# Two groups of six inner tiles in the channel mixer, and three VectorE-turned pairs in the second batch

## The chip, the cores and the metric

The kernel runs on one core of one Trainium2 chip. The metric is the device time of one execution in microseconds (us); the time of the kernel before is a median of three runs.

## What is computed

Three blocks follow each other, for a batch of 4 sequences of 448 positions. All inputs are float32, except the mixer's four weight matrices, which come as float64.

```
attention: 12 heads of 64; q, k rms-normed; softmax(q k^T / 8) v     -> x (4, 448, 768)
mixer:     u = x + (relu(x^T w_tok1) w_tok2)^T      w_tok1 448x256, w_tok2 256x448
           y = u + relu(u w_ch1) w_ch2              w_ch1 768x1536, w_ch2 1536x768
experts:   4 causal heads on y, gated by the 2 best of 4 logits, each with its own wo
```

## The kernel before

Heads are handled two at a time ("pairs"): six pairs (b,0) to (b,5) for each batch b. Every matrix product of the mixer is made of three matmuls on values split in two halves (high and low), 448 columns each, so that a product over K tiles of 128 is 3K matmuls on TensorE (PE), all recorded at L517.

**A pair's attention.** The scores (L599) come in two steps of two row blocks, VectorE (DVE) takes their maxima (L569), ScalarE (ACT) the exponentials (L584). The result must be turned before it can be multiplied with v (L722, "attend"). There are two ways. *Narrow* pairs are turned on PE: 28 transposes (L623) into four accumulators, which ACT or DVE copy out (L428 or L429). *Wide* pairs are turned by DVE: four stream transposes of 128x896 (L697), after which 16 copies between partition groups (L709), each on ACT, DVE or, for four of them, GpSimd (POOL), put the blocks in place. `LATE` names the first wide pair: every pair from it on, in order, is wide.

**The channel mixer** (`channel`, one call a batch). The 12 inner tiles of 128 are taken in `NG` groups of `GC`. For each group, PE makes `GC` inner tiles `hid` (L1088, 18 matmuls each: `a<-uhl,whl`), ACT or DVE takes relu (L433, L434), DVE the low half (L1095); then for each of the six output tiles PE makes a product over the group (L1102, 3 x GC matmuls: `a<-hid,whl`), which DVE adds to `u` (L1106). `RING` gives the number of buffers of a tile's ring: five for `hid`, six for the weights `whl`.

**Weights.** In the first batch each weight block is loaded as float64, in two halves (`narrow`): ACT takes two passes (L462, L465) and DVE two (L467, L469) to make float32 of a half; then `split` makes the high part (L428 or L429) and the low part (L447, on DVE or POOL) of each half, and both are stored in DRAM (L506). Later batches load the stored halves (L508).

**Order.** Every step has a cost and a list of engines that may run it. A list scheduler (`Plan.order`) lays all steps of the program out in time, chooses an engine where there is a choice, and the instructions are issued in that order. So a changed number moves rows on every engine. The pairs of batch b+1 are scored and turned while PE is in `channel(b)`: the pairs of batch 1 lie beside the first channel mixer, where the weights are prepared too. After it come the projection of batch 0 (`project`, L1123 and L1135) and the token mixer of batch 1, which needs the attention of all of batch 1's pairs.

Of the kernel before, what the change touches and what calls it, by code (L numbers as in the profile page):

```python
# [20 lines left out]


RING = {
    "w3": 3, "wraw": 2, "whl": 6, "hid": 5, "u": 6, "uhl": 6, "nat": 1,
# [17 lines left out]

FAST = {(0, 0), (0, 1)}

LATE = (1, 5)


class Buf:
# [268 lines left out]
def kernel(  # L317
# [40 lines left out]
    def sbuf(shape, dtype, tag):  # L358
        return plan.buf(sb, shape, dtype, tag, RING.get(tag, 1))
# [485 lines left out]
    class Stats:  # L845


        def __init__(self, b, qs, ks):
            n, m = len(qs), len(ks)
            self.b, self.qs, self.ks = b, qs, ks  # L850
            R = P if (b, max(qs + ks)) >= LATE else CP
            st = self.st = sbuf([R, 3, 64], F32, "st")
# [48 lines left out]
        def q(self, pr):  # L901
            o = self.at(0, pr)
            R = P if (self.b, pr) >= LATE else CP
            return self.st, lambda: self.st.t[:R, 1, o : o + 8].rearrange(
# [24 lines left out]
    class Pair:  # L929
# [10 lines left out]
        def stack(self):  # L940
# [3 lines left out]
            b, pr = self.b, self.pr  # L944
            wide = self.wide = (b, pr) >= LATE
            v = self.v = sbuf([P, NCH, 2, D], F32, "v")
# [279 lines left out]
def _layout(i):  # L1226
    import numpy as np

    b, h, s, d = i["q"].shape
    x = np.stack([i["q"], i["k"], i["v"]], axis=1).reshape(b, 3, h // 2, 2, s, d)  # L1230
    chunks = lambda y: y.reshape(b, h // 2, 2, 4, s // 4, d).transpose(0, 1, 4, 2, 3, 5)
    rows = lambda y: y.reshape(b, h // 2, 2, s // 4, 4, d).transpose(0, 1, 3, 2, 4, 5)
    kn = rows(x[:, 1]).copy()
    for at in FAST:
        kn[at] = chunks(x[:, 1])[at]
    qn = chunks(x[:, 0]).copy()
    late = [(i, j) for i in range(b) for j in range(h // 2) if (i, j) >= LATE]
    for at in late:
        qn[at] = rows(x[:, 0])[at]
    nat = np.stack([qn, kn], axis=3).reshape(b, h // 2, s // 4, 2, 2 * 4, d)  # L1240
    ends = [(0, 512 - s), (0, 0)]
    v = np.pad(x[:, 2], [(0, 0)] * 3 + ends)
    v[:, :, 1] = np.pad(x[:, 2, :, 1], [(0, 0)] * 2 + [ends[0][::-1], (0, 0)])
    vals = v.reshape(b, h // 2, 2, 4, 128, d).transpose(0, 1, 4, 3, 2, 5)
    qkt = x[:, :2].transpose(0, 2, 1, 3, 5, 4).reshape(b, h // 2, 2, 2 * d, s).copy()
    for at in late:
        qkt[at][0] = qkt[at][0].reshape(-1, s // 4, 4).swapaxes(-1, -2).reshape(-1, s)
    qkt = np.pad(qkt, [(0, 0)] * 4 + [(0, 16)])
    g = np.stack([i["g_q"], i["g_k"]], axis=1)
    gg = np.concatenate([g, g], axis=0)  # L1250
    t1, t2, c1, c2 = (
        np.ascontiguousarray(i["moe_w_" + n]).view(np.int64)
        for n in ("tok1", "tok2", "ch1", "ch2")
    )
    wt1 = t1.reshape(4, s // 4, -1).transpose(1, 0, 2).reshape(s // 4, -1)
    wt2 = t2.reshape(-1, 128, s).transpose(1, 0, 2).reshape(128, -1)
    dm, dc = c1.shape
    nd, ncc = dm // 128, dc // 128
    wc1 = c1.reshape(nd, 128, ncc, 128).transpose(2, 1, 0, 3).reshape(ncc, 128, dm)
    ng = 3  # L1260
    wc2 = (
        c2.reshape(ng, ncc // ng, 128, nd, 128).transpose(0, 3, 2, 1, 4)
        .reshape(ng, nd, 128, dc // ng)
    )
    e = i["moe2_wq"].shape[0]
    w = np.stack([i["moe2_wq"], i["moe2_wk"]], axis=0)
    w = w.reshape(2, e // 2, 2, nd, 128, d).transpose(1, 0, 4, 3, 2, 5)
    wqk = w.reshape(e, 128, dm)
    wv = i["moe2_wv"].transpose(1, 0, 2).reshape(dm, e * d)
    wvg = np.concatenate([wv, i["moe2_w_gate"]], axis=1)  # L1270
    wvg = wvg.reshape(nd // 2, 2, 128, -1).transpose(0, 2, 1, 3).reshape(nd // 2, 128, -1)
    wo = (
        i["moe2_wo"].reshape(e // 2, 2 * d, 2, dm // 2).transpose(2, 1, 0, 3)
        .reshape(2, 2 * d, e // 2 * (dm // 2))
    )
    return dict(nat=nat, qkt=qkt, vals=vals, gg=gg, wt1=wt1, wt2=wt2, wc1=wc1, wc2=wc2,
                wqk=wqk, wvg=wvg, wo=wo)
# [27 lines left out]
```

## Time and profile before

| | |
|---|---|
| time, median of 3 runs | 861.91 us (861.23 to 862.3) |
| profiled execution: time, span | 864.12 us, 862.3 us |
| PE busy | 823.4 us (95%) |
| DVE busy | 619.5 us (72%) |
| ACT busy | 468.0 us (54%) |
| POOL busy | 149.8 us (17%) |
| granted TensorE clock | full in all 40 slices |

The span is the time from the first to the last instruction of the profiled execution. Busy times are unions over an engine's instructions. The shares are means over stages that differ: the first 117 us (first batch's attention), the first channel mixer with the weights' preparation and the second batch's pairs (117 to 254 us), its projection, then three more rounds of the same with stored weights.

### The profile page before, as it was taken

The numbers are of one execution on the slowest core, as the hardware profiler recorded it, in microseconds if no ns is written. First come the engines' busy times: TensorE is split into PE (matmuls) and PEld (weight loads), VectorE is DVE, ScalarE is ACT, GpSimd is POOL, SyncE is SP. The second block draws the span as 40 slices with busy tenths as digits, with TensorE's granted clock in tenths as the row PEclk, the third lists the DMA queues.
The fourth block names the chain that finished last, engine by engine and source line by source line (L and its number), as shares of the span: only waits on it lengthen the run. The fifth ranks groups of instructions, "written<-read, shape, count | busy, mean of one in ns | idle before, by whom it ended". The sixth has DMA issues, their size and how long they took to land.

```text
span 862.3 us, 13533 instructions
## 1 busy us (share of the span) xinstructions
PE 823.4 (95%) x4564; PEld 636.1 (74%) x4564; DVE 619.5 (72%) x1341; ACT 468.0 (54%) x1077; POOL 149.8 (17%) x167
## 2 busy tenths in 40 slices
PE   3989999999989998999999998999999999999998
PEld 1446588777666876877776786788866789998786
DVE  6888988999999778646799877874389772125452
ACT  6898865577667546324395655641187631102443
POOL 3235640011123022020031211321031010000000
PEclk9999999999999999999999999999999999999999
DMA  8557769889878917687665614687656226676344
GB/s 249 165 156 208 221 187 297 275 266 308 254 230 230 312 67 233 187 270 233 174 192 158 188 47 138 206 224 209 197 160 160 91 71 186 211 239 206 106 136 165
DMA packets 109925, 168.40 MB, mean 195 GB/s; under 512 B 18112, under 2 KB 76608, under 8 KB 109856
## 3 DMA queue, kind: packets, MB, share of 16 engines
q1 hardware_dynamic: 109712, 167.54, 64.2%
q8 instruction: 36, 0.59, 0.3%
q14 instruction: 33, 0.27, 0.1%
q10 hardware_dynamic: 144, 0.00, 0.0%
HBM read 136.66 MB, written 30.84 MB: 194 GB/s over the span
## 4 chain that ended last, share of the span: by engine, by line
PE 73%; DVE 14%; DMA 5%; ACT 5%; issue 2%; SPq 0%; POOL 0%; ACTq 0%; DVEq 0%
PE a L517 52%; PE s L599 8%; PE m L722 8%; DVE nm L569 3%; ACT s L584 2%; PE m L748 2%; DMA w<-in_wc_dram 1%; DMA nat<-in_nat_dram 1%; PE s L647 1%; DVE wraw L467 1%; ACT s L428 1%; DVE s L709 1%; PE s L623 1%; DVE s L697 1%; DMA whl<-kept_c 1%
## 5 line engine op out<-in xcount | busy, mean ns | idle before, releaser
L517 PE MATMUL a<-uhl,whl 128*128 128x448 f32 x1152 | 242.5, 365 | 5.6 <-ACT ot L428 3.5
L517 PEld LDWEIGHTS a<-uhl,whl 128*128 128x128 f32 x1152 | 213.4, 188 | 35.2 <-issue 10.0
L517 PE MATMUL a<-hid,whl 128*128 128x448 f32 x864 | 187.0, 368 | 3.6 <-POOL whl L447 1.5
L517 PEld LDWEIGHTS a<-hid,whl 128*128 128x128 f32 x864 | 158.9, 188 | 31.1 <-issue 7.7
L584 ACT ACTIVATE s<-s,nm,st 128x448 f32<-128x448 f32 (+1 forms) x192 | 137.0, 724 | 65.1 <-DVE nm L575 41.8
L599 PE MATMUL s<-k,q 64*112 64x448 f32 (+4 forms) x512 | 112.4, 552 | 9.3 <-ACT s L584 6.6
L569 DVE TENSOR_REDUCE nm<-s 128x2 f32<-128x896 f32 (+1 forms) x96 | 101.7, 1082 | 10.4 <-PE s L599 10.1
L433 ACT ACTIVATE hid<-a 128x448 fp32r<-128x448 f32 x44 | 23.9, 543 | 131.1 <-PE a L517 131.0
L1095 DVE SCALAR_TENSOR_TENSOR hid<-a,hid 128x448 fp32r<-128x448 f32 x48 | 29.9, 622 | 75.8 <-ACT hid L433 75.5
L709 ACT COPY s<-s 32x896 f32<-32x896 f32 (+1 forms) x92 | 76.2, 829 | 9.8 <-DVE s L697 7.3
L722 PE MATMUL m<-s,v 128*64 128x448 f32 x384 | 77.5, 545 | 2.1 <-DVE s L709 1.1
L599 PEld LDWEIGHTS s<-k,q 64*112 64x112 f32 (+1 forms) x512 | 41.0, 184 | 48.8 <-issue 22.6
L1106 DVE TENSOR_TENSOR u<-a,u 128x448 f32<-128x448 f32 x72 | 44.3, 617 | 41.8 <-PE a L517 41.4
L447 POOL TENSOR_TENSOR uhl<-u,uhl 128x448 fp32r<-128x448 f32 x23 | 26.9, 1175 | 250.9 <-ACT uhl L428 131.5
L697 DVE STREAM_TRANSPOSE s<-s 128x896 f32<-128x896 f32 x52 | 55.6, 1094 | 14.1 <-ACT s L584 11.5
L709 DVE COPY s<-s 32x896 f32<-32x896 f32 (+1 forms) x87 | 59.9, 689 | 1.4
L722 PEld LDWEIGHTS m<-s,v 128*64 128x64 f32 x384 | 26.2, 136 | 44.0 <-issue 40.8
L584 ACT ACTIVATE s<-s,nm 112x112 f32<-112x112 f32 (+3 forms) x64 | 30.8, 492 | 28.3 <-DVE nm L563 28.1
L709 POOL COPY s<-s 32x896 f32<-32x896 f32 (+1 forms) x29 | 25.6, 882 | 94.6 <-DVE inv L669 53.5
L462 ACT ACTIVATE wraw<-w 128x256 f32<-128x256 f32 (+3 forms) x72 | 33.4, 464 | 15.6 <-DMA w<-in_wc_dram 15.3
L428 ACT ACTIVATE s<-s 112x448 f32<-112x448 f32 (+5 forms) x65 | 32.2, 539 | 16.2 <-PE s L647 11.2
L517 PE MATMUL a<-whl,uhl 128*112 128x260 f32 x288 | 39.9, 289 | 0.4 <-DVE q L545 0.4
(147 smaller groups left out, 1095.0 us busy)
## 6 DMA issues: line engine op xcount, KB each, us to landing
whl<-kept_c SPq DMA_DIRECT2D x72, 384.0 KB
whl<-kept_c SPq DMA_DIRECT2D x108, 256.0 KB
w<-in_wc_dram SPq DMA_DIRECT2D x24, 384.0 KB
kept_c<-whl SPq DMA_DIRECT2D x24, 384.0 KB
w<-in_wc_dram SPq DMA_DIRECT2D x36, 256.0 KB
kept_c<-whl SPq DMA_DIRECT2D x36, 256.0 KB
whl<-kept_qk SPq DMA_DIRECT2D x24, 384.0 KB
nat<-in_nat_dram SPq DMA_DIRECT2D x19, 448.0 KB
```

The lines of the kernel that those rows point to most:

```text
L428: lambda e: nc.scalar.activation(dst(), src(), AF.Copy) if e == "ACT"
L447: either(n, reads, writes, lambda e: e.tensor_tensor(dst()[:, 1], src(), f(dst()[:, 0]), op=ALU.subtract))
L462: add("ACT", act_ns(n), [(d, 1)], [(r, part)], lambda: nc.scalar.activation(rf(), half(1).bitcast(F32), AF.Copy, scale=2.0 ** -112))
L517: nc.tensor.matmul(acc, lhs[:, x], rhs[:, y], start=first and i == 0, stop=last and i == 2)
L569: lambda e: e.tensor_reduce(nm.t[:R, c], pst.t[:R, :, :w], axis=AX.X, op=ALU.max, negate=True))
L584: lambda j=j: nc.scalar.activation(s.t[:, c, j, :w], pst.t[:R, j, :w], AF.Exp, bias=nm.t[:R, c, j : j + 1], scale=-1.0 if rq is None else ...
L599: nc.tensor.matmul(pst.t[:R, j, :w], q.t[me, CP * c : CP * c + R], k.t[me, :w], start=True, stop=True)
L697: dve(2 * S + 64, [(s, (j, r)) for j in range(2)], [(t, r)], lambda e, r=r: e.transpose(t.t[:, :, 32 * r : 32 * r + 32], s.t[:, r].rearran ...
L709: lambda e, a=a, o=o, w=w, at=at: (nc.scalar.copy if e == "ACT" else ENG[e].tensor_copy)(at(p.t[32 * o : 32 * o + 32, :, P * a : P * a + N ...
L722: nc.tensor.matmul(av.t[64 * j : 64 * j + 64, q0:S], vat(j, c)[1](), p.t[:, j, c, q0:] if causal else p.t[:, 3 * j + c], start=c == 0, sto ...
L1095: lambda e, hl=hl, pa=pa: e.scalar_tensor_tensor(hl.t[:, 1], pa.t[:, :S], 0.0, f(hl.t[:, 0]), op0=ALU.max, op1=ALU.subtract))
L1106: dve(S, [pa], [u], lambda e, u=u, pa=pa: e.tensor_add(u.t, pa.t[:, :S], u.t))
```

## The change

Three numbers are changed, and one follows from the shape of `wc2` (`NG` 2, `GC` 6).

```diff
 RING = {
-    "w3": 3, "wraw": 2, "whl": 6, "hid": 5, "u": 6, "uhl": 6, "nat": 1,
+    "w3": 3, "wraw": 2, "whl": 6, "hid": 6, "u": 6, "uhl": 6, "nat": 1,
...
-LATE = (1, 5)
+LATE = (1, 3)
...
-    ng = 3
+    ng = 2
     wc2 = (
         c2.reshape(ng, ncc // ng, 128, nd, 128).transpose(0, 3, 2, 1, 4)
         .reshape(ng, nd, 128, dc // ng)
     )
```

The pairs (1,3) and (1,4) become wide, as (1,5) and all of batches 2 and 3 are already. Each channel mixer has two groups, so 12 products `a<-hid,whl` of 18 matmuls instead of 18 products of 12, and 12 additions to `u` instead of 18. The second weight's blocks become 128x768 instead of 128x512, and there are 12 and not 18 of them; a half is 384 wide instead of 256. The first weight's blocks were 128x768 before and stay.

Over the whole program the order of instructions shows these counts, before and after. PE: L623 into `s` 140 and 84; all L517 matmuls 2880 and 2880. DVE: L1106 72 and 48; L467 and L469 of 256 columns 36 each and none, of 384 columns 24 each and 48 each; L447 into `whl` of 256 columns 26 and none, of 384 columns 25 and 32; L429 into `whl` of 256 columns 26 and none, of 384 columns 23 and 38. POOL: L447 into `whl` of 256 columns 10 and none, of 384 columns 7 and 24; L709 of 32x896 18 and 25. Ahead of the last logit copy (L1140) of the first projection, DVE has 4 and then 12 L697; 6 and 14 L709 of 32x896; 2 and 5 of 32x448. All instructions of DVE are 1343 and 1292.

PE in the first channel mixer, before, at the place where pair (1,3) is turned (`s18` holds its exponentials, `hid8` to `hid11` are the last group's inner tiles, `k10` and `q10` belong to pair (1,4)):

```order
L517 MATMUL a79_2558<-hid11_2528,whl51_2578 128x448 x3
L623 MATMUL s56_2603<-ident_72,s18_2468 128x112 x8
L623 MATMUL s57_2615<-ident_72,s18_2468 128x112 x8
L517 MATMUL a80_2632<-hid8_2305,whl52_2585 128x448 x3
L623 MATMUL s58_2642<-ident_72,s18_2468 128x112 x8
L623 MATMUL s59_2659<-ident_72,s18_2468 128x112 x4
L517 MATMUL a80_2632<-hid9_2393,whl52_2585 128x448 x3
L517 MATMUL a80_2632<-hid10_2459,whl53_2653 128x448 x3
L517 MATMUL a80_2632<-hid11_2528,whl53_2653 128x448 x3
L599 MATMUL s60_2686<-k10_1217,q10_1232 112x448 x2
L599 MATMUL s61_2689<-k10_1217,q10_1232 112x448 x2
```

And now, at the second half of pair (1,4)'s scores (`hid6` to `hid11` are the second group's six inner tiles):

```order
L517 MATMUL a76_2522<-hid6_1931,whl44_2458 128x448 x3
L517 MATMUL a76_2522<-hid7_2017,whl44_2458 128x448 x3
L517 MATMUL a76_2522<-hid8_2072,whl44_2458 128x448 x3
L517 MATMUL a76_2522<-hid9_2121,whl45_2487 128x448 x3
L517 MATMUL a76_2522<-hid10_2202,whl45_2487 128x448 x3
L517 MATMUL a76_2522<-hid11_2288,whl45_2487 128x448 x3
L599 MATMUL s58_2580<-k10_1195,q10_1205 128x448 x2
L599 MATMUL s59_2583<-k10_1195,q10_1205 128x448 x2
L517 MATMUL a77_2604<-hid6_1931,whl46_2565 128x448 x3
```

The 28 transposes between products are gone, and a product holds its accumulator for 18 matmuls, where it was 12.

DVE at the maxima (L569 into `nm10`) of pair (1,4), before:

```order
L569 TENSOR_REDUCE nm10_2717<-s60_2686 112x2
L569 TENSOR_REDUCE nm10_2717<-s61_2689 112x2
L467 SCALAR_TENSOR_TENSOR wraw34_2715<-wraw34_2715,w368_2666 128x256
L575 TENSOR_TENSOR nm10_2717<-nm10_2717,st4_385 112x4
L469 SCALAR_TENSOR_TENSOR wraw34_2715<-w368_2666,wraw34_2715 128x256
L429 CAST whl56_2733<-wraw34_2715 128x256
L447 TENSOR_TENSOR whl56_2733<-wraw34_2715,whl56_2733 128x256
L1106 TENSOR_TENSOR u2_1212<-a80_2632,u2_1212 128x448
```

And now (`s18` to `s20` belong to pair (1,3)):

```order
L697 STREAM_TRANSPOSE s19_2400<-s18_2369 128x28x32 x2
L1106 TENSOR_TENSOR u2_1170<-a74_2428,u2_1170 128x448
L709 COPY s20_2505<-s19_2400 32x7x128
L569 TENSOR_REDUCE nm10_2519<-s56_2491 128x2
L569 TENSOR_REDUCE nm10_2519<-s57_2494 128x2
L709 COPY s20_2505<-s19_2400 32x7x64
L467 SCALAR_TENSOR_TENSOR wraw29_2498<-wraw29_2498,w358_2454 128x384
L575 TENSOR_TENSOR nm10_2519<-nm10_2519,st4_364 128x4
L467 SCALAR_TENSOR_TENSOR wraw29_2498<-wraw29_2498,w359_2474 128x384
L469 SCALAR_TENSOR_TENSOR wraw29_2498<-w358_2454,wraw29_2498 128x384
L469 SCALAR_TENSOR_TENSOR wraw29_2498<-w359_2474,wraw29_2498 128x384
L429 CAST whl46_2565<-wraw29_2498 128x384
```

The turning of pair (1,3) now stands on DVE around the next pair's maxima and among the weights' passes, which are fewer and wider.

## Rows read from the trace of the kernel before

**Rows 1.** Windows: us, busy (xinstructions) of PE, PEld, DVE, ACT, POOL, clock, DMA share, GB/s
```profile
0.00:117.00 117.00, 96.37 (x539) 54.34 (x540) 99.28 (x204) 93.30 (x223) 51.02 (x64) 1.00 0.70 197
117.00:254.00 137.00, 132.85 (x712) 103.50 (x712) 127.36 (x281) 92.34 (x219) 22.29 (x25) 1.00 0.82 264
254.00:293.00 39.00, 37.52 (x231) 28.44 (x229) 33.45 (x74) 23.92 (x62) 8.53 (x10) 1.00 0.89 257
```

**Rows 2.** The chain that ended last, in order of time: start, us, what
```profile
201.40 1.53 PE s L623 x16
...
205.96 1.15 PE s L623 x12
...
471.13 3.16 PE m L722 x16
...
482.91 3.23 PE m L722 x16
...
704.69 82.36 PE a L517 x411
```

**Rows 3.** Groups of 117 to 254 us: xcount, busy us, mean ns, idle before
```profile
L517 PE MATMUL a<-hid,whl 128*128 128x448 f32 x216 | 49.3, 373 | 3.4 <-POOL whl L447 1.5 <-DVE whl L447 1.0 <-DVE u L1106 0.8
L517 PE MATMUL a<-uhl,whl 128*128 128x448 f32 x219 | 46.7, 367 | 0.8 <-POOL whl L447 0.7
...
L623 PE MATMUL s<-ident,s 112*128 112x112 f32 x140 | 15.6, 259 | 0.0
```

**Rows 4.** The chain that ended last, between 254 and 284 us
```profile
279.14 0.74 DVE s L709
...
280.13 3.23 PE m L722 x16
```

**Rows 5.** Groups of DVE by shape, whole span: xcount, busy us, mean ns, idle before
```profile
L697 DVE STREAM_TRANSPOSE s<-s 128x896 f32<-128x896 f32 x52 | 55.6, 1094 | 14.1 <-ACT s L584 11.5 <-ACT s L709 2.1
...
L709 DVE COPY s<-s 32x896 f32<-32x896 f32 x73 | 53.0, 726 | 1.1
...
L1106 DVE TENSOR_TENSOR u<-a,u 128x448 f32<-128x448 f32 x72 | 44.3, 617 | 41.8 <-PE a L517 41.4
...
L469 DVE SCALAR_TENSOR_TENSOR wraw<-w,wraw 128x256 uint32<-128x256 uint32 x36 | 16.2, 450 | 0.8
L467 DVE SCALAR_TENSOR_TENSOR wraw<-wraw,w 128x256 uint32<-128x256 uint32 x36 | 16.0, 445 | 3.9 <-ACT w L465 3.0 <-ACT wraw L462 0.6
...
L467 DVE SCALAR_TENSOR_TENSOR wraw<-wraw,w 128x384 uint32<-128x384 uint32 x24 | 15.4, 644 | 0.3 <-ACT w L465 0.2
...
L447 DVE TENSOR_TENSOR whl<-wraw,whl 128x384 fp32r<-128x384 f32 x25 | 13.6, 553 | 0.3
...
L469 DVE SCALAR_TENSOR_TENSOR wraw<-w,wraw 128x384 uint32<-128x384 uint32 x24 | 13.2, 555 | 0.5
...
L447 DVE TENSOR_TENSOR whl<-wraw,whl 128x256 fp32r<-128x256 f32 x26 | 10.9, 420 | 0.4
...
L429 DVE CAST whl<-wraw 128x256 fp32r<-128x256 f32 x26 | 9.1, 350 | 0.8
...
L429 DVE CAST whl<-wraw 128x384 fp32r<-128x384 f32 x23 | 8.0, 355 | 0.5
...
L709 DVE COPY s<-s 32x448 f32<-32x448 f32 x14 | 6.9, 493 | 0.2
```

**Rows 6.** The same view, groups of POOL
```profile
L709 POOL COPY s<-s 32x896 f32<-32x896 f32 x18 | 18.0, 1002 | 37.9 <-DVE s L697 37.2
...
L447 POOL TENSOR_TENSOR whl<-wraw,whl 128x256 fp32r<-128x256 f32 x10 | 10.0, 996 | 48.0 <-DVE whl L429 36.5 <-DMA rn<-tni 5.6 <-PE s L599 3.9
L447 POOL TENSOR_TENSOR whl<-wraw,whl 128x384 fp32r<-128x384 f32 x7 | 7.2, 1034 | 50.6 <-DVE whl L429 39.1 <-issue 7.2 <-ACT whl L428 4.3
```

**Rows 7.** Timeline, POOL from 244 us: start, us, what
```profile
244.76 3.02 POOL L878 TENSOR_TENSOR nat<-nat 112x1024 f32<-112x1024 f32 x1
```

**Rows 8.** Timeline, DVE from 246 us
```profile
246.06 1.87 DVE L429 CAST whl<-wraw 128x256 fp32r<-128x256 f32 x1
```

## Prediction

> **What bounds the kernel now.** I read the busy times by stage first, because both edits act in one place: the first channel mixer, beside which batch 1's pairs are scored and turned and the weights are prepared. From 117 to 254 us PE is busy 132.85 of 137.0 us (97%) and DVE 127.36 (93%), while ACT has 92.34 and POOL 22.29 [rows 1]. So two engines are near their end at once: PE sets the pace, and DVE has only 9.6 us of room. From 254 to 293 us, in the projection, it is the same pair: PE 37.52 of 39.0, DVE 33.45. The first 117 us have PE busy 96.37 and DVE 99.28; nothing of the change belongs to that stretch but a few steps that the scheduler places otherwise.
>
> Next the chain that ended last. In the late, pure part of a channel mixer it is PE alone: 411 matmuls in 82.36 us, 0.200 us each [rows 2]. There DVE's work costs nothing. In the first channel mixer the chain passes through the transposes on PE: 16 in 1.53 us and 12 in 1.15 us [rows 2], nothing beside them on PE. Last, the end of batch 1's pairs: the attend of the last pair starts at 280.13 us, right behind a DVE copy of its turning at 279.14 [rows 4]; that is where DVE's length sets PE's time.
>
> **The change, part by part.**
>
> PE. A narrow pair's turning is 28 transposes, 1.53 + 1.15 = 2.68 us [rows 2]. Two pairs become wide: 56 of the 140 transposes go, 2 x 2.68 = 5.4 us. Scores and attends keep their number and their 448 columns, the mixer its matmuls. So PE's work falls by 5.4 us and by nothing else.
>
> DVE, ahead of the end of the first projection. Gone: 6 additions to u at 0.617 us, -3.7. The second weight's two passes: 36 x (0.445 + 0.450) = 32.2 us become 24 x (0.644 + 0.555) = 28.8, -3.4. Its high and low parts: 26 x (0.350 + 0.420) = 20.0 us go, and 15 casts at 0.355 and 7 subtractions at 0.553 come, 9.2, so -10.8. New: 8 stream transposes at 1.094, +8.8; 8 copies at 0.726 and 3 at 0.493, +7.3 (all durations [rows 5], the counts from the order of instructions). The sum is -17.9 + 16.1 = -1.8 us. The remaining differences on DVE there are single steps that the scheduler gives to another engine, both ways, and I take them as nothing. So DVE pays for the turning with what the wider blocks save, and is not the one to hold PE back, on the mean of the stage.
>
> POOL. 17 low parts at 1.034 come for 10 at 0.996, +7.6, and over the program 7 more copies at 1.002, +7.0 [rows 6]. POOL is busy 22.29 of 137 us [rows 1], so its own time is free; what its instructions do to DVE is a rival below. ACT has 44.7 us free in the stage [rows 1]. The weights' bytes stay the same (12 x 768 = 18 x 512 columns), and I take nothing from the transfers.
>
> PE's waits at the second products. In this stage the 216 matmuls `a<-hid,whl` take 49.3 us, 228 ns each, the 219 of `a<-uhl,whl` 46.7, 213 ns each [rows 3]: 15 ns x 216 = 3.2 us, and 3.4 - 0.8 = 2.6 us more idle time ahead of them, named after POOL's and DVE's low parts and the addition to u. That is 5.8 us that these waits cost more than the first products'. Three things ease them: the low parts are 24 and not 36, a product holds its accumulator for 18 and not 12 matmuls (3.6 and not 2.4 us by 0.200), and six weight buffers now hold half as many matmuls again. One speaks against: of the low parts of these widths POOL now makes 24 of 56, where it made 17 of 68, and it takes 1.034 us where DVE takes 0.553 [rows 5, 6]. The bounds are 0 and -5.8 us; nearest to me is the low end, since the slow maker of the parts gets more of them: -1 us.
>
> The sixth `hid` buffer. With six tiles a group and six buffers, the next group's first relu needs the buffer whose last reader is the first step of the group's last product, 15 matmuls from its end; PE makes 18 matmuls of a first product before that relu can start. So no wait. The last inner tile of a group is now wanted after 15 matmuls of the first product on it, 3.0 us, where it was 9, 1.8 us (0.200 each [rows 2]): more cover, not less.
>
> The other batches lose 6 additions each on DVE (3 x 3.7 us), in stages where PE's chain runs by itself [rows 2]: nothing.
>
> The new neighbours. Pairs (1,3), (1,4), (1,5) follow each other as wide pairs, with the tail as the risk. Batch 2 shows that such pairs can be attended 11.8 us apart, at 471.13 and 482.91 us [rows 2]; here the order leaves between the starts of the last two attends the first of them, 3.16 us, and 21 matmuls of 0.200 us, 7.4 us together [rows 2], and two halves of scores and 15 short matmuls beside them, so about as much. The tail fits, but has no room to spare. I take +1 us for waits there, between 0 and the full 5.4.
>
> **Sum.** The span was 862.3 us: 862.3 - 5.4 - 1 + 1 = 856.9. The profiled execution gives 864.12 us as its own time, 1.8 above its span; the median of the runs is 861.91, 0.4 below that span, and it is the median that I compare with: 856.9 - 0.4 = **856.5 us**.
>
> **Rivals.** What cannot be told from no change is some 0.2%, 1.7 us: faster is below 860.2, slower above 863.6.
>
> *DVE is locked out by POOL (slower).* Beside a POOL instruction of 3.02 us from 244.76 us, a DVE cast that takes 0.350 us on the mean took 1.87 [rows 5, 7, 8]: 1.5 us lost, and it ends as POOL's 3.02 us end is near. POOL gets 14.6 us more (above), most of it among DVE's casts and copies. If each of these microseconds stopped DVE for one, DVE's stage would be 14.6 - 1.8 = 12.8 us longer against its room of 9.6; PE would lose 3.2 us at the pace of DVE, 862.3 + 3.2 - 0.4 = 865.1. It decides from 1.8 us on (DVE longer than before), and turns the sign once DVE's excess passes 9.6. For it speaks that one row; against it, that the casts' means with POOL running in all stages are still 0.350 and 0.355, that is most of them meet nothing. The Trainium skill (SBUF — State Buffer, "Who interferes with whom") says that DVE and GpSimd share one pair of ports under an exclusive lock, which a two-port copy or a DVE instruction with two SBUF inputs takes for its whole length, so that the second to come blocks; this case's row of 1.87 us agrees with that, and by the rule every copy of the turning can also hold up POOL's low parts.
>
> *The transposes become waits (no change).* The turning of (1,3) and (1,4) and the last pair's tail lie on DVE. If the wait at 280 us [rows 4] only moves by DVE's 1.8 us, PE arrives 5.4 us sooner and waits 3.6: 862.3 - 1.8 - 0.4 = 860.1; with the copies of (1,4) crowded into the tail, where the order now puts more of DVE's turning than before, the rest goes too, some 861.5. For it: the chain is DVE's there. Against: DVE got shorter as well, and PE has the projection's products to fill with. The Trainium skill (VectorE: DVE Perf Modes, "Rules for kernel authors") gives a 128x128 transpose to TensorE where a PSUM destination will do, and DVE's only for 32x32 blocks; that speaks against this change. The rows agree as to the price of one pair: 2.68 us on PE against 4 x 1.094 = 4.4 us on DVE before a single copy [rows 2, 5].
>
> *The waits at the second products go too (faster yet).* All 5.8 us with the 5.4: 862.3 - 11.2 - 0.4 = 850.7.
>
> **Chances.** The forecast, 856.5 with a range of its own of 853 to 860: 0.49. Both gains: 0.13. Transposes become waits: 0.17. POOL's lock: 0.21. So faster 0.62, same 0.17, slower 0.21. The range has to leave out no more than 2 in 10: from 851.0, which keeps most of the third rival, to 865.0, the price of the lock.
>
> **What will show it.** L623 into `s` 84 times and some 9.4 us busy instead of 15.6 [rows 3]. In the first channel mixer DVE's busy time within 2 us of before over the same work, and the attend of pair (1,5) some 5 us sooner than 280.1; if it is less than 2 sooner, the second rival holds. The mean of `a<-hid,whl` in that stage at or below 228 ns. DVE's means of L709 and L429 as before (0.726, 0.355); if they are up by a tenth or more, it is the lock. I am wrong if PE stalls at places that have nothing to do with the edits, because the scheduler laid every batch anew: that I can't price from these rows, and a shift of several us in batches 2 or 3 would be its mark.

## The result, and the profile after

The changed kernel takes **872.1 us** (867.62 to 873.21, 6 runs) against 862.09 of the kernel before beside it: ratio 1.0113 [1.0088, 1.0139]. It is slower by some 10 us; forecast was 856.5, faster by 5.4, and 872.1 lies above the range of 851 to 865. The profiled execution took 870.81 us, span 868.9: 6.7 us above the profiled execution of before (864.12). The medians are 10 us apart because the profiled execution of before lay 2 us above its median and that of the changed kernel 1.3 below. What follows explains the 6.7 us.

Windows of the same three stretches, with the columns of [rows 1]:

```profile
0.00:117.00 117.00, 94.61 (x528) 52.21 (x528) 99.34 (x191) 90.86 (x217) 43.95 (x57) 0.96 0.65 193
117.00:254.00 137.00, 132.15 (x670) 102.88 (x671) 128.30 (x243) 94.08 (x201) 36.23 (x34) 0.99 0.85 267
254.00:293.00 39.00, 36.94 (x223) 27.44 (x222) 35.23 (x79) 29.93 (x67) 13.15 (x15) 1.00 0.88 251
```

The busy times of PE and DVE hardly moved; the granted clock is no longer 1.00 throughout. Busy shares of fixed stretches don't tell when a stage ends, so I read the starts of three matmuls from the trace: the first of the first channel mixer, the last of its projection, and the last of all. Between them lie three parts, here called start-up, stage and rest:

| profiled execution | start-up | stage | rest |
|---|---|---|---|
| before | 117.3 | 175.4 | 565.7 |
| after | 122.7 | 170.4 | 572.1 |
| difference | +5.4 | -5.0 | +6.4 |

The stage, where both edits act, became shorter by 5.0 us, nearly the 5.4 of the forecast. The loss is in the two other parts, on which the prediction had put nothing. The attend of pair (1,5), which was to come some 5 us sooner than 280.1, starts at 279.26 us, 0.9 sooner; measured from the start of the stage it comes 6.2 us sooner.

In the stage, groups of PE between 117 and 254 us (columns of [rows 3]):

```profile
L517 PE MATMUL a<-uhl,whl 128*128 128x448 f32 x222 | 48.2, 370 | 0.0
L517 PE MATMUL a<-hid,whl 128*128 128x448 f32 x216 | 46.3, 370 | 0.2 <-DVE u L1106 0.2
L623 PE MATMUL s<-ident,s 112*128 112x112 f32 x84 | 9.3, 260 | 0.6 <-ACT s L428 0.6
```

The transposes are 84 in 9.3 us, as forecast. The second products take 46.3 / 216 = 214 ns each where they took 228, and wait 0.2 us where they waited 3.4: less than the first products' 217. By this measure, the prediction's own, the 5.8 us that they cost beyond those are gone, all of them.

The chain that ended last (start, us, what) is not PE's everywhere. First the end of the start-up, then the end of the stage, then the pure stretch of the last mixer:

```profile
114.12 0.11 DVE st L834
...
114.26 1.18 DVE st L838
...
115.46 1.09 DVE st L841
...
118.27 0.21 DVE st L843
118.48 0.34 DVE h L1059
118.83 0.04 issue
118.87 7.26 PE a L517 x28
...
266.94 2.32 ACT s L584 x7
...
274.15 4.18 DMA rn<-inv
278.35 0.50 SPq L685
278.90 3.87 DMA rn<-rn
...
287.36 1.69 PE a L517 x12
...
710.21 85.42 PE a L517 x417
```

And what PE itself does at these places (timeline of PE: start, us, line, idle before in brackets), and then the window from 118.3 to 121.8 us, with the granted clock in the last column but two:

```profile
112.41 3.01 PE L517 MATMUL a<-xhl,t 112*128 112x256 f32 x24 [0.58 <-DVE u L1077]
115.25 0.93 PE L748 MATMUL m<-ident,xn 112*128 112x112 f32 x8
118.87 4.02 PE L517 MATMUL a<-t,h 128*128 128x448 f32 x12 [2.69 <-DVE h L1059]
...
275.40 1.34 PE L517 MATMUL a<-whl,uhl 128*112 128x260 f32 x9 [0.94 <-ACT q L543]
...
287.36 0.85 PE L517 MATMUL a<-whl,uhl 128*112 128x260 f32 x5 [0.75 <-DVE lg L1140]
```

```profile
118.30:121.80 3.50, 2.93 (x8) 2.64 (x9) 2.06 (x5) 0.00 (x0) 0.00 (x0) 0.51 0.16 18
```

Before, the same end of the start-up reads:

```profile
114.31 0.88 PE L517 MATMUL a<-t,h 128*128 128x448 f32 x3 [0.70 <-DVE h L1059]
115.02 0.55 PE L748 MATMUL m<-ident,xn 112*128 112x112 f32 x4
115.33 2.18 PE L517 MATMUL a<-t,h 128*128 128x448 f32 x9
```

Three things are to be seen.

- At 114 us eleven DVE steps on the next batch's statistics (`st`) stand ahead of the token mixer's L1059, and PE waits 2.69 us for that. In this wait, at 118.3 us, the granted clock falls to its lower level, 1.2 GHz, until 121.8 (0.51 of full on the mean).
- From 267 to 287 us the chain is not PE's: a wide pair's exponentials, its turning, and two DMAs one behind the other, 8.05 us, that spread the pair's row sums. But PE has other work beside nearly all of it: where the chain comes back to PE, at 287.36 us, PE has waited 0.75 us. So this chain's length is not PE's loss.
- In the pure stretch 417 matmuls take 85.42 us, 204.8 ns each, where [rows 2] has 411 in 82.36, 200.4 ns: the same instruction is slower by 2%, with nothing between and a granted clock of 1.00 both times.

Over the program the mean spacing from start to start of neighbouring matmuls of one kind (spacings under 300 ns) went from 202.5 to 205.5 ns for `a<-hid,whl` (864 matmuls) and from 200.9 to 204.1 for `a<-uhl,whl` (1152): 2.6 + 3.7 = 6.3 us. The two small kinds `a<-xhl,whl` and `a<-h,whl`, 36 matmuls each, went from a median of 201 to 206 ns. Kinds that take their weights from elsewhere kept theirs (medians: `a<-xhl,t` 114 and 114 ns, `a<-h,w` 203 and 203), so it is not the clock. What the slower kinds share is that their weights lie in `whl`. In the compiled programs this ring starts at byte 146336 of a partition before, 32 beyond a multiple of 128, and at 178656 after, 96 beyond one: the new order takes the tiles into use in another sequence, and that decides where they lie.

### The profile page after: what moved, and what is told of

It is laid out like the page before. It is cut to its first block, busy times and chain, and to the rows that moved or that the text cites. A ratio compares the mean times of both kernels' runs of the same rounds, so it can differ in the third digit from the quotient of the medians.

```text
span 868.9 us, 13161 instructions
## 1 busy us (share of the span) xinstructions
PE 826.2 (95%) x4508; PEld 632.9 (73%) x4508; DVE 622.5 (72%) x1290; ACT 465.5 (54%) x1046; POOL 157.7 (18%) x173
## 4 chain that ended last, share of the span: by engine, by line
PE 71%; DVE 14%; DMA 6%; ACT 5%; issue 2%; SPq 1%; ACTq 0%; DVEq 0%
PE a L517 51%; PE s L599 8%; PE m L722 8%; DVE nm L569 3%; ACT s L584 3%; DMA nat<-in_nat_dram 1%; DVE s L697 1%; PE m L748 1%; PE s L647 1%; DMA w<-in_wc_dram 1%; PE a L623 1%; DVE s L709 1%; DVE wraw L467 1%; DMA rs<-st 1%; DVE wraw L469 1%
## 5 line engine op out<-in xcount | busy, mean ns | idle before, releaser
L517 PE MATMUL a<-uhl,whl 128*128 128x448 f32 x1152 | 247.3, 369 | 3.5 <-ACT ot L428 3.5
L517 PEld LDWEIGHTS a<-uhl,whl 128*128 128x128 f32 x1152 | 213.3, 188 | 38.4 <-issue 10.6
L517 PE MATMUL a<-hid,whl 128*128 128x448 f32 x864 | 185.6, 370 | 1.6 <-DVE u L1106 1.5
L517 PEld LDWEIGHTS a<-hid,whl 128*128 128x128 f32 x864 | 160.6, 188 | 27.0 <-issue 7.0
L599 PE MATMUL s<-k,q 64*128 64x448 f32 (+4 forms) x512 | 113.5, 556 | 7.8 <-ACT s L584 6.4
L569 DVE TENSOR_REDUCE nm<-s 128x2 f32<-128x896 f32 (+1 forms) x96 | 101.1, 1080 | 11.0 <-PE s L599 10.5
L709 ACT COPY s<-s 32x896 f32<-32x896 f32 (+1 forms) x97 | 82.8, 853 | 6.1 <-DVE s L697 4.5
L433 ACT ACTIVATE hid<-a 128x448 fp32r<-128x448 f32 x39 | 21.2, 544 | 120.3 <-PE a L517 120.1
L1106 DVE TENSOR_TENSOR u<-a,u 128x448 f32<-128x448 f32 x48 | 29.8, 620 | 60.5 <-PE a L517 60.2
L709 DVE COPY s<-s 32x896 f32<-32x896 f32 (+1 forms) x104 | 71.1, 684 | 1.8
L697 DVE STREAM_TRANSPOSE s<-s 128x896 f32<-128x896 f32 x60 | 63.4, 1089 | 8.8 <-ACT s L584 7.2
L447 POOL TENSOR_TENSOR uhl<-u,uhl 128x448 fp32r<-128x448 f32 x27 | 32.3, 1203 | 126.7 <-DVE uhl L429 50.4
L447 POOL TENSOR_TENSOR whl<-wraw,whl 128x384 fp32r<-128x384 f32 (+1 forms) x29 | 31.9, 1105 | 101.1 <-DVE whl L429 46.0
L709 POOL COPY s<-s 32x896 f32<-32x896 f32 (+1 forms) x39 | 34.0, 872 | 80.9 <-DVE s L697 66.6
L517 PE MATMUL a<-whl,uhl 128*112 128x260 f32 x288 | 39.9, 288 | 1.8 <-ACT q L543 0.9
L428 ACT ACTIVATE s<-s 112x448 f32<-112x448 f32 (+5 forms) x52 | 23.8, 498 | 32.9 <-PE s L647 30.0
```

The lines of the kernel that those rows point to most:

```text
L428: lambda e: nc.scalar.activation(dst(), src(), AF.Copy) if e == "ACT"
L433: lambda e: nc.scalar.activation(dst(), src(), AF.Relu) if e == "ACT"
L447: either(n, reads, writes, lambda e: e.tensor_tensor(dst()[:, 1], src(), f(dst()[:, 0]), op=ALU.subtract))
L517: nc.tensor.matmul(acc, lhs[:, x], rhs[:, y], start=first and i == 0, stop=last and i == 2)
L569: lambda e: e.tensor_reduce(nm.t[:R, c], pst.t[:R, :, :w], axis=AX.X, op=ALU.max, negate=True))
L599: nc.tensor.matmul(pst.t[:R, j, :w], q.t[me, CP * c : CP * c + R], k.t[me, :w], start=True, stop=True)
```

## The experiments

Each was timed in five rounds beside the kernel before; chips differ (before is 861.8 to 865.2 us), so the ratios are to be compared. Start-up, stage and rest are of one profiled execution each, in us.

| run | wide pairs of batch 1 | groups | median | ratio [95%] | start-up | stage | rest |
|---|---|---|---|---|---|---|---|
| e1 whl moved back | 3, 4, 5 | 2 | 867.54 | 1.0061 [1.0037, 1.0086] | 124.6 | 168.2 | 568.4 |
| e2 before, whl moved | 5 | 3 | 867.88 | 1.0071 [1.0044, 1.0098] | 114.7 | 177.3 | 568.9 |
| e3 groups alone | 5 | 2 | 855.78 | 0.9924 [0.9901, 0.9948] | 117.1 | 168.1 | 565.2 |
| e4 LATE alone | 3, 4, 5 | 3 | 860.39 | 0.9985 [0.9966, 1.0003] | 112.6 | 175.5 | 563.5 |
| e5 root moved | 3, 4, 5 | 2 | 866.97 | 1.0059 [1.0041, 1.0077] | 120.2 | 168.6 | 571.7 |
| e6 root, whl as before | 3, 4, 5 | 2 | 863.78 | 1.0023 [1.0001, 1.0045] | 120.6 | 168.9 | 567.0 |
| e8 both, new order | 3, 4, 5 | 2 | 863.32 | 1.0021 [1.0006, 1.0037] | 123.8 | 172.5 | 565.6 |
| e9 both, new order | 3, 4, 5 | 2 | 867.43 | 1.0062 [1.0042, 1.0082] | 121.7 | 172.2 | 567.5 |
| e10 before, new order | 5 | 3 | 871.21 | 1.0086 [1.0054, 1.0117] | 121.7 | 178.1 | 561.8 |
| e11 both, less DVE | 3, 4, 5 | 2 | 864.48 | 1.0003 [0.9978, 1.0027] | 124.5 | 168.3 | 566.6 |
| e12 groups, more DVE | 5 | 2 | 873.58 | 1.0109 [1.0086, 1.0132] | 120.1 | 185.0 | 562.8 |
| e13 groups, new order | 5 | 2 | 858.1 | 0.9927 [0.9904, 0.9951] | 119.6 | 167.9 | 563.9 |
| e14 other place | 1, 2, 5 | 2 | 875.88 | 1.011 [1.0073, 1.0147] | 122.7 | 179.8 | 567.8 |
| e15 its new order | 1, 2, 5 | 2 | 866.91 | 1.002 [0.9993, 1.0047] | 126.1 | 171.8 | 565.7 |
| e16 no wide at the end | 1, 2 | 2 | 875.25 | 1.01 [1.0058, 1.0142] | 133.8 | 173.0 | 563.7 |
| e17 LATE (1,4) | 4, 5 | 2 | 866.33 | 1.0005 [0.9981, 1.0028] | 123.6 | 169.5 | 563.6 |

**Where whl lies (e1, e2).** `SHIFT` puts a tile of 64 bytes ahead of a ring; the order of instructions stays. e1 moves `whl` in the changed kernel by 64 bytes to 32 beyond a multiple of 128 (`hid` goes up by 128 bytes, `uhl` stays), e2 moves it in the kernel before to 96 (`uhl` and `hid` stay).

```diff
-SHIFT = {"t1", "h1", "uhl"}
+SHIFT = {"t1", "h1", "uhl", "whl", "hid"}   # e1, in the changed kernel
+SHIFT = {"t1", "h1", "whl"}                 # e2, in the kernel before
```

> The changed kernel, instruction for instruction in the same order, with one unused 64-byte tile allocated ahead of the weights' ring whl and one ahead of hid, so that whl starts at 32 modulo 128 bytes, as in the kernel before (the changed kernel has it at 96, like uhl). Address theory: the matmuls that take weights from whl run at 200 us per thousand again (a<-hid,whl median 200 ns, now 205; a<-uhl,whl mean below 300 ns 200.9, now 204.1), 6.7 us less over 2088 matmuls: about 865.4 us. Rival, another chip or clock: nothing moves, 872 us and 205 ns. Rival, the new order of steps alone: 870 us or more.

> The kernel before, in the same order, with the unused tile ahead of whl and not ahead of uhl: whl at 96 modulo 128 bytes, uhl and hid where they were. Address theory: the pace of the matmuls from whl falls to some 205 ns and the time rises by 6 to 7 us, 868.6 us. Rival, the pace belongs to the chip or the order: 861.9 us and 200 ns.

e2, with not one instruction moved, is 0.71% slower than the kernel before; its spacing is 206.6 ns for `a<-hid,whl` and 204.3 for `a<-uhl,whl`. In the chain of its pure stretch 411 matmuls take 203.8 ns each, where [rows 2] has 200.4:

```profile
705.39 83.77 PE a L517 x411
```

e1 is 4.6 us faster than the changed kernel by the medians, not the 6.7 expected; spacing 202.4 and 202.8 ns. So the address is a cause of about half of the loss, shown in both directions. With e1's place it is not all of it.

**One part alone (e3, e4).** e3 is the kernel before with `ng = 2` and `hid` 6, e4 with `LATE = (1, 3)`; `whl` stays at a multiple of 128 plus 32 in both.

> Two groups of six and six hid buffers, LATE as before (one wide pair in batch 1); whl comes to lie at 32 modulo 128. If the groups alone gain, as the prediction had it: 861.9 less 1 to 3 us. If the new order of steps costs by itself: 864 to 868 us. Clock 1.0 if the clock falls because of the pairs, below if because of the groups.

> LATE (1,3) alone, three groups of four, five hid buffers; whl lies at 32 modulo 128. By the prediction 861.9 - 5.4 and up to 5 us of waits: 857 to 862 us. If the turning costs DVE more than PE gains: 863 to 868 us. The transposes into s 84 times at 96 ns either way.

The groups are the gain: stage 168.1 for 175.4, 0.76% faster than before, more than expected. `LATE` alone changes the stage by 0.1 us (175.5). Counted by the starts of PE's matmuls, its transposes take 7.8 us there for 12.8, but PE's waits are 8.7 us for 5.6, and from 163.5 to 166.9 us, at a granted clock of 0.51, nine `a<-uhl,whl` are spaced by some 373 ns and not 201, which costs 1.6 us. In e3's groups of PE between 117 and 254 us the second products show about half of the gain that they have with both edits:

```profile
L517 PE MATMUL a<-uhl,whl 128*128 128x448 f32 x240 | 51.0, 366 | 0.1
L517 PE MATMUL a<-hid,whl 128*128 128x448 f32 x216 | 46.9, 369 | 2.0 <-DVE hid L1095 2.0
```

They take 217 ns each for the first products' 212, and wait 2.0 us: 2.9 us are left of the 5.8. PE's waits in e3's whole stage are 2.0 us, before 5.6. And 1.4 us of the 7.3 come from 16 transposes that e3's order does ahead of the stage. In e4's, where groups are of four, they take 223 ns, with 3.8 us of waits, and the first products wait for DVE too:

```profile
L517 PE MATMUL a<-hid,whl 128*128 128x448 f32 x216 | 48.1, 371 | 3.8 <-DVE u L1106 1.8 <-DVE whl L429 1.5 <-POOL whl L447 0.5
L517 PE MATMUL a<-uhl,whl 128*128 128x448 f32 x214 | 48.0, 377 | 3.2 <-DVE hid L1095 3.2
```

And e3's chain at the end of the stage is PE's own, with no wait from 251.81 to 289.27 us (some of its lines):

```profile
254.92 2.60 PE a L517 x12
257.52 3.16 PE m L722 x16
260.68 1.40 PE a L517 x6
...
270.76 3.16 PE m L722 x16
...
286.86 2.41 PE a L517 x21
```

**The start-up (e5), and the whole of whl's place (e6).** e5 is e1 with the root of `st` issued behind the last L1059 of batch 0's token mixer; e6 puts `whl` 384 bytes further up still (its expectation says 432), so that it lies to `uhl` as in the kernel before (64 beyond a multiple of 512 apart).

```diff
-        for k in self.order():
+        out = self.order()
+        i, j = out.index(self.root), out.index(self.edge)
...
+        out[i : j + 1] = rest + moved
+        for k in out:
...
-                self.pool.tile([128, 16], F32, tag="by" + self.tag, name="by" + self.tag, bufs=1)
+                w = 112 if self.tag == "whl" else 16   # e6
+                self.pool.tile([128, w], F32, tag="by" + self.tag, name="by" + self.tag, bufs=1)
```

> The changed kernel with whl moved (as e1), and on DVE the eleven steps of the root of batch 1's second group of statistics (st) put behind the last L1059 of batch 0's last token mixer instead of between its h12 and h13. Theory A (the start-up loss is this root, which PE waits for through L1059 of h13): the first matmul of the first channel mixer comes some 4 us sooner than in e1 (124.6 us), near 120, and the time falls from e1's 867.5 to 863 to 864 (0.995 to 0.996 of e1), about the kernel before's. Rival B (the first 120 us are longer for another reason, such as the stretches at half the granted clock or the order of the weights' preparation): the first channel mixer starts at 123 us or later and the time stays at 866 to 869. Rival C (what is gained there is waited for at the next landmark, since the weights of the mixer are not ready): the mixer starts near 120, and its last projection matmul still stands near 293 us, time 866 to 868.

> As e5, with whl another 432 bytes further up, so that whl stands to uhl (64 mod 512 bytes) and at 416 mod 512 as in the kernel before. Theory A (the pace of a matmul goes by where whl lies against the tiles it is multiplied with): the spacing of a<-uhl,whl is 200.9 ns again (e1: 202.8), that of a<-hid,whl stays near 202.5, and the time is some 2 us below e5's, 861 to 862. Rival (only whl's offset mod 128 counts): spacing as e1's 202.8 and time as e5's.

In e5 PE starts the mixer at 120.2 us, not 124.6, and the root's steps, off PE's way, take 0.19 to 0.29 us each and not up to 1.18. But the median is 0.6 us below e1's, within the intervals, and the trace shows the gain handed back, which comes nearest to rival C: e5's projection ends at 288.8 us, e1's at 292.8, and the last of the next mixer's second products starts at 450.2 and 450.5. Besides, e11 below has the root in e5's place and starts at 124.5. Theory A is not borne out; a start-up of one order varies by some 4 us between executions or with small things. e6 came as expected in its spacing, though not down to 861 to 862 us: `a<-uhl,whl` at 201.1 ns again (e5 202.7), 3.2 us faster than e5, and the pure stretch at 200.3 ns a matmul:

```profile
703.89 83.54 PE a L525 x417
```

With e1 and e6 together the address was worth 872.1 - 863.8 = 8.3 us (7.8 by the ratios); the root's share of it is the 0.6 of e5, not told from nothing.

**The same work in another order (e8, e9, e10, e13).** `LAG` is a number that only the planner uses; 205 or 195 in place of 200 lays every batch anew.

```diff
-    LAG = {"PE": 200, "ACT": 170, "DVE": 150, "POOL": 250, "SP": 2400}
+    LAG = {"PE": 205, "ACT": 170, "DVE": 150, "POOL": 250, "SP": 2400}   # e8 after, e13 groups alone
+    LAG = {"PE": 195, "ACT": 170, "DVE": 150, "POOL": 250, "SP": 2400}   # e9 after, e10 before
```

> The changed kernel with the planner's lag of PE at 205 and not 200, which does nothing but lay the steps in another order: the root of batch 1's second group of statistics comes ahead of h12's L1059, and whl lies at the good place (uhl minus whl 64 mod 512 bytes). Theory A: the first channel mixer starts near 115 to 119 us, the spacing of its matmuls is 201 to 202.5 ns, and the time is 855 to 860, below the kernel before: both edits as such are good for some 5 us, and the loss of the changed kernel was the place of two things. Rival B (transposes by VectorE and groups of six cost DVE what they save PE): 865 to 870 whatever the place.

> The changed kernel with the planner's lag of PE at 195: whl at a good place, but the root of batch 1's second group of statistics between L1059 of h12 and of h13, as in the changed kernel. Theory A (root): matmul spacing 201 to 202.5 ns, the first channel mixer starts at 121 to 125 us, and the time is 3 to 5 us above that of the lag of 205, some 861 to 865. Rival (start-up goes by something else): it starts where it does with the lag of 205, within 1.5 us.

> The groups of six alone with the planner's lag of PE at 205, that is the same work laid in another order, whl at a good place. Theory A (the gain of the groups is that of DVE's and PE's shorter waits, not of one lucky order): 854 to 859, at least 3 us below the kernel before. Rival B (e3's gain is its order): 860 to 866.

> The kernel before with the planner's lag of PE at 195: nothing but another order, with whl at the same place. It tells how far a new order alone moves the time. Theory A (an order alone is worth up to some 3 us, mostly in the first 120 us, and the edits the rest): 859 to 865. Rival B (orders scatter by as much as the edits, 6 us and more): 866 or above, or 857 or below.

In all four `whl` lies at the better place. e10, the kernel before without any edit, loses 0.86% by its new order: in the profile 4.4 us in the start-up and 2.7 in the stage, with 3.9 won back in the rest; the medians say more. So an order alone is worth as much as these edits; that is rival B of its expectation. The groups alone keep their gain in both orders (0.9924 and 0.9927, stages 168.1 and 167.9). Both edits are no faster than before in either new order, and their stages are 172.5 and 172.2 us; e8 lies between its two expectations, e9 above both of its own; e8 has the root ahead of h12's L1059 and starts the mixer at 123.8 us, no sooner than e9, which has it in the way, at 121.7 (e8's profiled execution, 867.49 us, is its longest): the root by itself falls as the cause.

**Is it DVE's length? (e11, e12).** e11 is e6 with L469's pass over the second weight on 32 of 384 columns, e12 is e3 with that pass done twice.

```diff
-            ru(), half(1), 0x80000000, ru(), op0=ALU.bitwise_and, op1=ALU.bitwise_or), port=True)
+            ru()[:, :m], half(1)[:, :m], 0x80000000, ru()[:, :m],              # e11, m = 32
+            op0=ALU.bitwise_and, op1=ALU.bitwise_or), port=True)
...
+            for _ in range(2 if again else 1)][-1], port=True)                 # e12
```

> The kernel with both edits, root and whl moved (e6), in its order, with one thing less: L469's OR of the sign runs on 32 and not 384 columns for the 24 halves of the second weight, so those weights keep only part of their signs. That takes some 24 x 0.57 = 14 us from DVE in and around the first channel mixer and nothing from PE. Theory A (with both edits DVE sets the pace there, so that the 56 transposes that PE no longer does became waits for DVE): from the first matmul of the first channel mixer to the last of the projection it takes 161 to 164 us instead of e6's 168.9, and the time falls from 863.8 to 856 to 859. Rival B (DVE has room; the loss is made in the first 120 us and in waits between single steps): 167 to 169 us there, and a time of 862 or more.

> The groups of six alone (e3), in its order, with L469 done twice for the 24 halves of the second weight, which changes no value: 24 x 0.644 = 15.5 us more for DVE, about what the turning of two pairs costs it (16.1 us), and PE keeps its transposes. Theory A (DVE's length sets the stage): the stretch of the first channel mixer and projection grows from 168.1 us by 5 to 9, and the time from 855.8 to 861 to 865. Rival B: DVE's time is hidden there, 855 to 857.5.

They answer against each other. e12's stage grows by 16.9 us, more than the work put in (some 15 us); for 10.2 us of it the granted clock was 0.50, with matmuls spaced by 373 ns, which costs an estimated 4 us. Its waits of PE between 120 and 306 us (us in total, times, longest) name DVE, the low halves of `hid` and the additions to `u`:

```profile
PE a L518 <- DVE hid L1096: 4.4, 1, 4.4
PE a L518 <- DVE u L1107: 4.0, 3, 2.0
```

e11 took less from DVE than expected, since a pass on 32 columns is not that short; its row among the groups of DVE, from 124 to 293 us:

```profile
L478 DVE SCALAR_TENSOR_TENSOR wraw<-w,wraw 128x32 uint32<-128x32 uint32 x24 | 6.3, 265 | 0.5
```

Against the 0.607 us that the full pass has on the mean in e6's stage that is 24 x 0.342 = 8.2 us. e11's stage is 168.3 us and e6's 168.9: 8.2 us less on DVE bring next to nothing, where 4 or more should have come if each held PE back. So DVE's total is not what holds both edits back. Nor is the serial end shown to: e11's chain there reads as that of the changed kernel, with two DMAs of 5.04 and 3.50 us, and PE's wait at its end is 1.27 us.

**Other places for the wide pairs (e14 to e17).** If the serial end of three wide pairs in a row were the cost all the same, other places should be better. A set takes the place of the comparison with `LATE`; all have groups of six, `whl` at the better place.

```diff
-LATE = (1, 5)
+WIDE = {*((1, 1), (1, 2), (1, 5)), *((b, p) for b in (2, 3) for p in range(6))}   # e14, e15 (LAG 205)
+WIDE = {*((1, 1), (1, 2)), *((b, p) for b in (2, 3) for p in range(6))}           # e16
+WIDE = {*((1, 4), (1, 5)), *((b, p) for b in (2, 3) for p in range(6))}           # e17
```

> Groups of six, and three wide pairs in batch 1 as in the changed kernel, but (1,1), (1,2), (1,5) instead of (1,3), (1,4), (1,5); whl at a good place. Theory T (a serial tail of three wide pairs in a row eats the transposes' gain): first channel mixer to last projection matmul 162 to 165 us, against 168.1 with the groups alone, the chain at the end of the stage mostly PE's, and a time of 850 to 854 if the first 120 us are as before. Rival V (turning on VectorE as such eats it): 168 to 170 us and a time of 856 to 864.

> As the kernel with wide pairs (1,1), (1,2), (1,5), in another order (lag of PE 205). Theory T: the stage again 162 to 165 us. Rival V: 168 to 170 us. If the two orders differ by more than 3 us in that stage, scatter of the orders is the answer, and no place of the pairs is better than another by these runs.

> Groups of six, wide pairs (1,1) and (1,2) alone in batch 1; the last pair (1,5) is turned by PE. PE's work is that of one pair's transposes, 2.7 us, less than with the groups alone. Theory T: 164 to 167 us in the stage, no wait for the last pair's spread DMA at its end, time 851 to 855. Rival V: as with the groups alone or longer, 168 and more, 856 or more.

> Groups of six and LATE (1,4): half of the second edit, two wide pairs in a row at the end. Theory T: PE's 2.7 us are eaten in part, 166 to 169 us in the stage, time 854 to 858. Rival V: 168 to 170 us, 856 to 860. If it lies 3 us or more under the groups alone, the third wide pair in a row is what costs.

Theory T fails: all four take longer than the groups alone (866.3 to 875.9 us), and the stage is 179.8 and 171.8 us in two orders of one choice, 173.0 without a wide pair at the end, 169.5 with two. The two orders differ by 8 us there, so by their own expectation no place of the pairs is better than another by these runs. What holds is narrower: no kernel with one or two more wide pairs in batch 1 came below 168.2 us in the stage, whatever it took from PE.

## Why the prediction was wrong

**The transposes: the work right, the gain wrong.** "PE's work falls by 5.4 us" holds for the transposes (84, 9.3 us). But that it arrives as time does not: alone it leaves the stage at 175.5 for 175.4 (e4), and beside the groups at 168.2 to 168.9 (e1, e5, e6) for 168.1 (e3), or at 172.5 and 172.2 in other orders (e8, e9). So the step that failed is the +1 us taken for waits, "between 0 and the full 5.4": the upper end was right. The mechanism is in part that of the rival "the transposes become waits", which had 0.17: in e4 PE waits 3.1 us more in the stage, most of it for DVE. But the place is not the one that this rival and the forecast named, the tail of the last pairs: PE's wait ahead of the attend of pair (1,5) was 1.1 us before and is 0.5 after. With groups of six, e1's waits are 4.2 us for e3's 2.0, and its scores take 20.4 us for 19.2. What makes up the rest, and whether another order would spare it, stays open. The Trainium skill (VectorE: DVE Perf Modes, "Rules for kernel authors") gives a 128x128 transpose to TensorE where PSUM will do. With groups of six the runs side with it: e3, which leaves these two pairs to TensorE, has a ratio of 0.9924, e6 1.0023; with groups of four e4 can't be told from no change.

**The waits at the second products: mis-sized.** -1 us was taken, "nearest to me is the low end, since the slow maker of the parts gets more of them". By the prediction's measure the term is the other bound, -5.8, with both edits, and -2.9 in e3; counted by the starts of PE's matmuls it is -4.1 and -2.7. POOL's share of the low parts, 24 of 56, did not keep it small. That -5.4 in all was forecast for the stage and -5.0 came is luck: two errors, the waits and this term, about cancel.

**DVE and the lock.** DVE's busy time in the stage is 128.30 for 127.36 us, within the 2 us named. The sign for the lock did show: over the program L429 into `whl` of 384 columns takes 15.8 / 38 = 0.417 us for 0.355, up by more than a tenth, while L709 has 0.740 for 0.726. These are the groups of DVE in the profile after (columns of [rows 5]):

```profile
L709 DVE COPY s<-s 32x896 f32<-32x896 f32 x80 | 59.2, 740 | 1.4
...
L429 DVE CAST whl<-wraw 128x384 fp32r<-128x384 f32 x38 | 15.8, 417 | 1.0
```

38 x 0.062 = 2.4 us in all, and e8, where that cast takes 0.364 us, has no shorter stage (172.5). So the sign named for the lock is seen, and it does not decide; that the lock is what makes the cast longer no run here tells apart.

**"Nothing of the change belongs to that stretch": failed.** The first 117 us were priced at nothing but steps placed otherwise. The changed kernel loses 5.4 us there in the profile: 2.3 up to the last 24 `a<-xhl,t` (112.41 us for 110.12), 2.0 by the longer wait for L1059 behind the root (2.69 us for 0.70), and 1.1 by the last 12 `a<-t,h`, of which six are spaced by 373 ns in a stretch with a granted clock of 0.51. None of these is the cause by itself: e8 and e9 speak against the root, and e9 has a granted clock of 1.00 to 120 us and starts at 121.7. What about these orders makes the start-up long stays open. It need not be the edits: e10 loses 4.4 us there without any.

**The mixers' matmuls: the term that was missing.** The prediction let "the mixer its matmuls" keep 0.200 us each. They take 3 ns more, 6.3 us by their spacing; 4.7 of it lie in the rest, which grew by 6.4, and 1.6 in the stage. The medians of e1 and e6 give 4.6 and 8.3 us. This is the largest single cause of the slower kernel, and it comes from an address, not from the work.

**The granted clock: put at nothing, and not settled.** On the mean of all timed executions it is 0.990 for the changed kernel, 0.990 to 0.993 for e1, e4, e5, e6, e8 and e9, 0.995 to 0.998 for the kernel before on the four chips, and 0.998 for the groups alone (e3, e13). So, to the question in e3's expectation, it falls with the wide pairs and not with the groups; but it is low without them too, 0.989 in e10 and 0.991 in e12. An estimate of the most that it can be worth between e6 (0.9902) and e3 (0.9978): 2 x 0.0076 x 860 = 13 us more at half the clock, of which matmuls spaced by 373 ns for 201 lose 0.46, 6 us. For the kernel before, its cost isn't seen: timed with e1 to e4 its executions at 1.000 took 859.45 to 864.26 us, those at 0.990 to 0.994 took 859.48 to 864.48. No run sets the clock apart from the order.

The account of the profile, by the starts of PE's matmuls: start-up +5.4; stage -5.0 (transposes -5.0, second products with their waits -4.1, scores with theirs +2.7, waits in the projection +1.4; the address is in these with 1.6); rest +6.4 (4.7 of it the address); together +6.8, the span +6.6. That "the scheduler laid every batch anew" was named as what would make the forecast wrong, and "a shift of several us in batches 2 or 3" as its mark; but it got no price and no chance of its own, and nor did an address. That put 872 outside the range.

Faster than both kernels are the groups of six alone: 855.78 and 858.1 us in two orders.

## What to carry to other kernels

Where a scheduler orders the instructions and a pool lays out the buffers, a changed number is three changes: the work, the order, and the addresses. Time the old work in a second order before believing a gain below 1%, and compare the spacing of an unchanged instruction before and after, which tells an address in one line. Work taken from the busiest engine can come back as waits for the engine that gets it: e4 took 5.0 us from PE's transposes, PE waited 3.1 us more, and the stage stayed. And a chain that leaves an engine for 20 us can stand for a wait of 0.75 us: read the engine's own idle time beside it.

## What the runs showed of the hardware that was not expected

A matmul of 128x128 by 448 columns repeats, at a granted clock of 1.00, every 200 or every 205 ns (medians), by where the buffers of its operands lie in SBUF. On the mean, with the `whl` ring 32 bytes beyond a multiple of 128, `a<-hid,whl` has 201.7 to 203.0 ns in sixteen kernels; with 96, 205.5 and 206.6 (after, e2). `a<-uhl,whl` has 200.7 to 201.1 where `uhl` lies 64 bytes beyond `whl` by multiples of 512, 202.7 and 202.8 at 448 (e1, e5), 204.1 and 204.3 at 0 (after, e2). Whether the weights' own address counts or the distance to the operand they meet was not told apart.

A DVE step on 112x48 elements takes 0.22 us, and 1.18 or 1.09 us in the changed kernel at 114 us, while two POOL subtractions into `uhl` ran from 114.24 to 116.48 us beside them. e1, with the same instructions, shows the same two steps at 1.19 and 1.08 us from 115.82, beside POOL's from 115.81 to 118.06. That POOL is what holds them up was not tested by itself.
